# Loading order at the start of a fused Fourier and feed-forward kernel: first table behind x on SyncE, second tile on ScalarE's queue

## The chip, the cores and the metric

The kernel runs on one core of a Trainium2 chip. The metric is the time of one execution on the device, in microseconds (us); the time before is the median of 3 runs.

## The reference

```python
batch, seq, dim = (8, 3008, 256)               # x
X = np.fft.fft(x, axis=1)
X = np.fft.fft(X, axis=2)
x = X.real.reshape(24064, 256)
h = x @ w_in                                   # 256 x 2048
r = np.maximum(h, 0.0)
return (r * r @ w_out).astype(np.float32)      # 2048 x 256
```

## The kernel before

Each of 8 batches is a Fourier transform along 3008 rows and 256 columns, followed by two matrix products with a squared ReLU between them. The transform along the rows is a product with tables of cosines and sines. Symmetries make the tables small: the rows of x are regrouped on the host in sets of four mirrored rows (`x` has the shape batch, row, 4, 256), VectorE adds and subtracts the four ("folding"), and only a quarter of the rows is multiplied. The transform along the columns is folded into the first weights (`win`), so that a block of the steady loop multiplies the row transforms `Pt` and `Qt` with `G` (line 1101), forms and squares the ReLU on VectorE, ScalarE and GpSimd, and multiplies with the second weights (line 1166). That loop runs from about 40 us to the end.

The change lies in the head, which prepares batch 0. The rows are cut into seven tiles (`TILES`); tile t has a row of x in each partition, four vectors of 256 each. They are used in the order 0, `ODD0` (number 4), 1, 5, 2, 3, 6. For each, `load_x` brings x, `load_table` brings the cosines, `turn_table` makes the sines on ScalarE (line 234), `fold...` folds on VectorE, and `products_of` multiplies on TensorE (lines 811 and 824). Tile 0 has 95 rows in use and is loaded in two halves; its folding is `fold_first`: lines 583 and 584 for each half, 593 and 595 for both, while ScalarE makes turned copies for the first products (lines 588, 589, 591). Tile `ODD0` is loaded in two halves too; `fold_begun` uses the first in lines 604 and 605 and the second in line 606, then lines 607 and 609, and `fold_rest` goes on with lines 620 to 623. Later tiles are folded in lines 560 to 569.

The order of the work on each engine is the order in which the program is written out; nothing reorders it. SyncE's queue (SPq) issues nearly all loads, one after the other; ScalarE and GpSimd (POOL) have queues of their own, and an issue there stands in line with the engine's other instructions. The table `cosT` of tile 0 comes in three pieces of 32 rows (95 columns for each of two parities), the table of `ODD0` in one piece of 128 rows and 377 columns. Each DMA of SyncE and ScalarE completes on one of eight semaphores, which are taken in turn, and the DMA that takes one again is issued only when the one before it has landed.

`awake(n)` runs n products of a blank tile on TensorE (line 263; each shows as two records). `nc.scalar.copy(turn[0:1, 0, 0:1], ident[0:1, 0:1])`, line 1397, is ScalarE's first computation, ahead of which its function table is loaded; `nc.gpsimd.tensor_copy(turn[0:1, 0, 1:2], xt[0, 0][0:1, 3, 0:1])`, line 1398, makes GpSimd wait for tile 0 before it issues the table of tile 1 and the sines of tile 0.

Of the kernel before, what the change touches and what calls it, by code (L numbers as in the profile page):

```python
# [39 lines left out]
def row_tiles(S):  # L40

    q = S // 4
    tiles, at = [], 0
    for count in (q // 2 + 1, q // 2):
        assert 2 * P < count <= 3 * P
        for r in range(0, count, P):
            tiles.append((at + r, min(P, count - r)))
        at += count
    return tiles
# [35 lines left out]
def kernel(  # L85
# [12 lines left out]
    nc = tc.nc  # L98
# [42 lines left out]
    xt = {}  # L141
# [3 lines left out]
    ODD0 = NT - 3  # L145
# [15 lines left out]
    def later_rows(t):  # L161

        if t >= ODD0:
            return [(p, S // 8 + 1 + first, count, 1) for p, first, count in ODD[t - ODD0]]
        c, r0, step, rows = TILES[t]
        if t == TWO + 1:
            return [(p, TILES[TWO][1] + step * (2 * HALF2 - p - R), R, step) for p in range(0, ROWS2, R)]
        return [(0, r0, rows, step)]

    def load_x(b, t, parts_=4):  # L170
        if b and (t >= ODD0 or t == TWO + 1):
            xt[b, t] = xp.tile([P, 4, D], F32, name="xt", tag="x")
            for p, first, count, step in later_rows(t):
                nc.sync.dma_start(out=xt[b, t][p:p + count], in_=x[b, first:first + step * (count - 1) + 1:step])
            return
        c, r0, step, rows = TILES[t]

        if b == 0:
            rows, src = P, x.rearrange("b r i d -> (b r) i d")[r0:r0 + step * (P - 1) + 1:step]
        else:  # L180
            while rows % 15 and rows % 16 and r0 + step * rows < NROW:
                rows += 1
            src = x[b, r0:r0 + step * (rows - 1) + 1:step]

        pool, tag = (gp, "g") if b == 0 and t < NT - NX else (xp, "x")
        xt[b, t] = pool.tile([P, 4, D], F32, name="xt", tag=tag)
        for i in range(0, 4, parts_):
            nc.sync.dma_start(out=xt[b, t][0:rows, i:i + parts_],
                              in_=src[:, i:i + parts_])

    LATER = [(b, t) for b in range(1, B)
             for t in (TWO, TWO + 1, 0, *(() if b > 1 else (1,)), *range(ODD0, NL), *((1,) if b > 1 else ()))]
# [1 line left out]
    def load_later(i):  # L194
        if i < len(LATER):
            load_x(*LATER[i])
# [3 lines left out]
    cosT, sinT = ([const.tile([P, 2, WT], F32, name=nm), sp.tile([P, 2, WL], F32, name=nm + "l", tag="s")]  # L200
                  for nm in ("cosT", "sinT"))

    def part_of(tab, t):
        return tab[t in LATE]
# [3 lines left out]
    ident = const.tile([P, P], F32, name="ident")  # L208
# [5 lines left out]
    def load_table(tab, src, tiles, queue=nc.sync):  # L214

        for t in tiles:
            c, r0, step, rows = TILES[t]
            for i, (s0, count) in enumerate(row_tiles(S)):
                mine = [r for r in range(count) if (s0 + r - r0) % step == 0 and 0 <= (s0 + r - r0) // step < rows]
                if mine:  # L220
                    o, m = (s0 + mine[0] - r0) // step, len(mine)
                    while (step == 1 or m % 15) and m % 16 and o + m < P and mine[0] + step * m < P:
                        m += 1
                    nk = NC[0][c]
                    queue.dma_start(out=part_of(tab, t)[o:o + m, :, PLACE[t]:PLACE[t] + nk],
                                    in_=src[mine[0]:mine[0] + step * (m - 1) + 1:step, :, i, 0:nk])

    def turn_table(t):


        c, at, rows = TILES[t][0], PLACE[t], TILES[t][3]
        for kp in range(2):
            nk = NC[kp][c]
            nc.scalar.mul(part_of(sinT, t)[0:rows, kp, at:at + nk], part_of(cosT, t)[0:rows, kp, at:at + nk][:, ::-1],
                          sind[0:rows, 0, P - 1:])
# [24 lines left out]
    def awake(n):  # L260
        filled = psh.tile([P, CH], F32, name="filled", tag="h")
        for _ in range(n):
            nc.tensor.matmul(filled[:, 0:P], blank, blank, start=True, stop=True)
# [157 lines left out]
    turn = const.tile([P, 3, 4], F32, name="turn")  # L421
# [963 lines left out]
    def products_of(names):  # L1385
        for nm in names.split():
            (p_part if nm[0] == "P" else q_part)({"P": "", "Q": "", "E": "e"}[nm[0]] + nm[1:])

    start()
    load_table(cosT, cos_s, (0,), nc.scalar)  # L1390
    awake(11)
    load_x(0, 0, 2)
    load_x(0, ODD0, 2)
    load_table(cosT, cos_s, (ODD0,))
    load_x(0, 1)
    load_x(0, ODD0 + 1)
    nc.scalar.copy(turn[0:1, 0, 0:1], ident[0:1, 0:1])
    nc.gpsimd.tensor_copy(turn[0:1, 0, 1:2], xt[0, 0][0:1, 3, 0:1])
    load_table(cosT, cos_s, (1,), nc.gpsimd)
    load_table(sinT, sin_s, (0,), nc.gpsimd)  # L1400
# [12 lines left out]
    first = round_win(0, raw["in", 0])  # L1413
    fold_first()
    products_of("P0 E0")
    awake(2)
    turn_table(ODD0)
    fold_rest(ODD0, *fold_begun(ODD0))
    products_of("P4 E4 Q4")
# [219 lines left out]
    i = 0  # L1639
# [17 lines left out]
    for i in range(PLAIN, len(steps) + 2):  # L1657
        if i < len(steps):
            b, k0, n, j = steps[i]
# [130 lines left out]
```

## Time and profile before

| | |
|---|---|
| median of 3 runs | 1855.04 us (1854.84 to 1855.18) |
| profiled execution | 1855.63 us, span 1853.8 us |
| granted TensorE clock | 0.999 |
| DMA engines, mean | 70.10 MB, 38 GB/s |
| TensorE's first product, line 811 | at 6.46 us |

The profile shows one execution: times count from the start of the span, PE is TensorE, PEld its weight loads, DVE is VectorE, ACT ScalarE. A group of instructions is shown with its number, busy time and what ended the idle time before it. The time of the profiled execution is 1.83 us more than the span, and 0.59 us more than the median of the runs.

### The profile page before, as it was taken

The numbers are of one execution on the slowest core, as the hardware profiler recorded it, in microseconds if no ns is written. First come the engines' busy times: TensorE is split into PE (matmuls) and PEld (weight loads), VectorE is DVE, ScalarE is ACT, GpSimd is POOL, SyncE is SP. The second block draws the span as 40 slices with busy tenths as digits, with TensorE's granted clock in tenths as the row PEclk, the third lists the DMA queues.
The fourth block names the chain that finished last, engine by engine and source line by source line (L and its number), as shares of the span: only waits on it lengthen the run. The fifth ranks groups of instructions, "written<-read, shape, count | busy, mean of one in ns | idle before, by whom it ended". The sixth has DMA issues, their size and how long they took to land.

```text
span 1853.8 us, 33923 instructions
## 1 busy us (share of the span) xinstructions
PE 1846.4 (100%) x11336; PEld 1746.8 (94%) x11336; DVE 1473.9 (80%) x3481; ACT 1076.3 (58%) x1596; POOL 1458.5 (79%) x2132
## 2 busy tenths in 40 slices
PE   9999999999999999999999999999999999999999
PEld 7699999999999999999999999999999999999998
DVE  8998788887788878788788887788878887767666
ACT  5785555665556655657456664565645666444454
POOL 3499778788788887888778887788877888787885
PEclk9999999999999999999999999999999999999999
DMA  7441011110111101111011100111001100000010
GB/s 223 109 61 43 19 25 47 41 29 23 32 32 46 30 18 32 43 39 27 15 32 46 49 15 15 46 45 36 15 21 46 35 15 21 19 20 15 21 43 23
DMA packets 153987, 70.10 MB, mean 38 GB/s; under 512 B 132608, under 2 KB 144717, under 8 KB 153813
## 3 DMA queue, kind: packets, MB, share of 16 engines
q1 hardware_dynamic: 153173, 67.58, 14.4%
q8 instruction: 91, 1.49, 0.3%
q14 instruction: 83, 0.68, 0.1%
q10 hardware_dynamic: 384, 0.20, 0.0%
q0 software_dynamic: 256, 0.15, 0.0%
HBM read 43.18 MB, written 24.69 MB: 37 GB/s over the span
## 4 chain that ended last, share of the span: by engine, by line
PE 98%; DVE 1%; ACT 0%; DMA 0%; issue 0%; POOL 0%; SPq 0%; DVEq 0%; ACTq 0%
PE F L1166 34%; PE S L1166 23%; PE hQ L1101 17%; PE hP L1101 17%; PE pd L947 1%; PE mA L1195 1%; PE mB L1195 1%; PE pd L921 1%; PE pd L824 1%; PE pg L360 1%; PE ph L1069 0%; PE ph L1074 0%; PE fin L1277 0%; DMA xt<-in_x_dram 0%; DVE w L569 0%
## 5 line engine op out<-in xcount | busy, mean ns | idle before, releaser
L1114 ACT ACTIVATE g<-g 128x1008 f32<-128x1008 f32 (+1 forms) x384 | 399.4, 1040 | 303.2 <-DVE g L1110 278.5
L1105 DVE SCALAR_TENSOR_TENSOR he<-ew,gE,hP 128x252 f32<-128x252 f32 (+1 forms) x748 | 321.3, 471 | 284.6 <-PE hP L1101 284.5
L1117 ACT ACTIVATE g<-g 128x1008 f32<-128x1008 f32 (+1 forms) x384 | 399.4, 1040 | 12.0
L1101 PE MATMUL hQ<-Qt,G 128*128 128x252 f32 (+3 forms) x1496 | 378.7, 376 | 0.4 <-ACT g L1114 0.2
L1101 PE MATMUL hP<-Pt,G 128*128 128x252 f32 (+1 forms) x1496 | 378.1, 375 | 0.0
L1166 PE MATMUL F<-s,wsum 128*128 128x168 f32 (+1 forms) x1496 | 335.4, 306 | 0.0
L1101 PEld LDWEIGHTS hQ<-Qt,G 128*128 128x128 f32 (+1 forms) x1496 | 282.3, 190 | 36.2 <-ACT g L1114 2.0
L1166 PE MATMUL F<-g,wout 128*128 128x168 f32 (+1 forms) x1496 | 304.1, 305 | 0.0
L1139 POOL TENSOR_TENSOR s<-g 128x168 f32<-128x168 f32 (+1 forms) x187 | 101.3, 542 | 251.1 <-ACT g L1117 133.5
L1109 DVE TENSOR_TENSOR g<-he,hQ 128x504 f32<-128x504 f32 (+1 forms) x374 | 252.9, 676 | 39.3 <-DVE he L1105 2.7
L1101 PEld LDWEIGHTS hP<-Pt,G 128*128 128x128 f32 x1496 | 266.2, 190 | 17.6 <-issue 0.7
L1166 PE MATMUL S<-s,wout 128*128 128x168 f32 (+1 forms) x1496 | 280.3, 306 | 0.0
L1166 PE MATMUL S<-s,wsum 128*128 128x168 f32 (+1 forms) x1496 | 273.7, 306 | 0.0
L1166 PE MATMUL F<-g,wsum 128*128 128x168 f32 (+1 forms) x1496 | 273.5, 305 | 0.0
L1110 DVE TENSOR_TENSOR g<-he,hQ 128x504 f32<-128x504 f32 (+1 forms) x374 | 251.0, 671 | 0.0
L1166 PEld LDWEIGHTS F<-s,wsum 128*128 128x128 f32 x1496 | 247.5, 190 | 0.0
L1166 PEld LDWEIGHTS S<-s,wsum 128*128 128x128 f32 x1496 | 239.1, 190 | 8.5 <-issue 0.5
L1166 PEld LDWEIGHTS F<-g,wsum 128*128 128x128 f32 x1496 | 239.3, 190 | 8.1
L1166 PEld LDWEIGHTS F<-g,wout 128*128 128x128 f32 x1496 | 239.3, 190 | 0.0
L1166 PEld LDWEIGHTS S<-s,wout 128*128 128x128 f32 x1496 | 230.9, 190 | 0.7 <-issue 0.5
L1142 POOL TENSOR_TENSOR s<-s 128x336 f32<-128x336 f32 (+1 forms) x187 | 168.5, 901 | 14.7
L1145 POOL TENSOR_TENSOR s<-s 128x336 f32<-128x336 f32 (+1 forms) x187 | 167.8, 898 | 14.7
(246 smaller groups left out, 2474.6 us busy)
## 6 DMA issues: line engine op xcount, KB each, us to landing
out_dram<-os SPq DMA_DIRECT2D x376, 56.0 KB
xt<-in_x_dram SPq DMA_DIRECT2D x35, 384.0 KB
xt<-in_x_dram SPq DMA_DIRECT2D x63, 128.0 KB
raw<-in_moe_w_out_dram SPq DMA_DIRECT2D x20, 256.0 KB
ew<-e_dram SPq DMA_DIRECT2D x39, 126.0 KB
out_dram<-os SPq DMA_DIRECT2D x288, 7.0 KB
raw<-in_moe_w_in_dram SPq DMA_DIRECT2D x16, 256.0 KB
xt<-in_x_dram SPq DMA_DIRECT2D x5, 512.0 KB
```

What stands on the lines that cost most here:

```text
L360: nc.tensor.matmul(pg, tab[:, i], win[j][:, i], start=i == 0, stop=i == 1)
L1101: nc.tensor.matmul(to[:, h, 0:n], w[:, fs], v[:, ks], start=h == 0, stop=True, skip_group_check=True)
L1105: nc.vector.scalar_tensor_tensor(out=t[:, h, 0:n], in0=window[b, k0][:, 0:n], scalar=gE[:, fc:fc + 1], in1=hP[:, h, 0:n], op0=ALU.mult, op ...
L1109: tt(out=g[:, :, 0:n], in0=t[:, :, 0:n], in1=hQ[:, :, 0:n], op=ALU.add)
L1110: tt(out=g[:, :, n:2 * n][:, :, ::-1], in0=t[:, :, 0:n], in1=hQ[:, :, 0:n], op=ALU.subtract)
L1114: act(g[:, :, 0:2 * n], g[:, :, 0:2 * n], AF.Relu)
L1117: act(g[:, :, 0:2 * n], g[:, :, 0:2 * n], AF.Square)
L1139: gt(out=s[:, 11], in0=b2[:, 0], in1=b1[:, 0], op=SUB)
L1142: gt(out=s[:, 4:6], in0=s[:, 4:6], in1=s[:, 10:11].to_broadcast([P, 2, tb]), op=SUB)
L1145: gt(out=s[:, 6:9:2], in0=s[:, 2:4], in1=s[:, 6:8], op=ADD)
L1166: nc.tensor.matmul(acc[nm][:, slot, 0:tb], w, v, start=q == 0 and nm not in begun, stop=q == end - 1, skip_group_check=True)
L1195: nc.tensor.matmul(acc[nm][:, 0:2 * n], wout[:, j, h, c], g[:, c, 0:2 * n], start=j == c == 0, stop=j == NJ - 1 and c == 1)
```

## The change

In the head, tile 0 of x is loaded with 96 rows instead of 128. The first table's three pieces go from ScalarE's queue, where they were the first instructions, to SyncE's queue behind tile 0. ScalarE's first copy, and with it its function table, stands ahead of two DMAs that ScalarE now issues: the halves of tile `ODD0`, which SyncE issued before. The fillers ahead of the first products are 9 instead of 11, and the two ahead of the products of `ODD0` are left out.

```diff
-    def load_x(b, t, parts_=4):
+    def load_x(b, t, parts_=4, queue=nc.sync):
...
-        if b == 0:
+        if b == 0 and t:
             rows, src = P, x.rearrange("b r i d -> (b r) i d")[r0:r0 + step * (P - 1) + 1:step]
         else:
             while rows % 15 and rows % 16 and r0 + step * rows < NROW:
...
-            nc.sync.dma_start(out=xt[b, t][0:rows, i:i + parts_],
-                              in_=src[:, i:i + parts_])
+            queue.dma_start(out=xt[b, t][0:rows, i:i + parts_], in_=src[:, i:i + parts_])
...
     start()
-    load_table(cosT, cos_s, (0,), nc.scalar)
-    awake(11)
+    awake(9)
     load_x(0, 0, 2)
-    load_x(0, ODD0, 2)
-    load_table(cosT, cos_s, (ODD0,))
+    nc.scalar.copy(turn[0:1, 0, 0:1], ident[0:1, 0:1])
+    load_x(0, ODD0, 2, nc.scalar)
+    load_table(cosT, cos_s, (0, ODD0))
     load_x(0, 1)
     load_x(0, ODD0 + 1)
-    nc.scalar.copy(turn[0:1, 0, 0:1], ident[0:1, 0:1])
     nc.gpsimd.tensor_copy(turn[0:1, 0, 1:2], xt[0, 0][0:1, 3, 0:1])
...
     products_of("P0 E0")
-    awake(2)
     turn_table(ODD0)
```

## The prediction

> **What bounds the kernel now.** I read the page's busy shares and chain first, then the chain in order of time for the first 30 us, then stretches, the timeline and the DMA queues of the first 10 us.
>
> ```profile
> PE 1846.4 (100%) x11336; PEld 1746.8 (94%) x11336; DVE 1473.9 (80%) x3481; ACT 1076.3 (58%) x1596; POOL 1458.5 (79%) x2132
> PE 98%; DVE 1%; ACT 0%; DMA 0%; issue 0%; POOL 0%; SPq 0%; DVEq 0%; ACTq 0%
> ```
>
> TensorE is busy 1846.4 of 1853.8 us, so everything that is not matmul time amounts to 7.4 us, head and tail together. A change of the head can win only part of that.
>
> The chain, in order of time (start, length, what):
>
> ```profile
> 0.75 0.41 SPq L188
> 1.22 4.32 DMA xt<-in_x_dram
> 5.56 0.42 DVE fs L583
> ...
> 7.37 0.33 DVE fs L604
> 7.70 0.34 DVE fd L605
> 8.04 0.35 DVE fs L606
> ```
>
> Until 5.56 the end is set by the second half of x's first tile (called x0b here; x0a is the first half, x4a and x4b are the halves of the tile ODD0, which is number 4). From 5.56 to about 23.5 VectorE folds tile after tile without a gap, then GpSimd's fold of the last tile and its conversion of weights release TensorE at 28.19. From 39 us on TensorE alone counts. So the step that can move the end is when VectorE may start, and whether it then runs on. In the stretches (PE, PEld, DVE, ACT, POOL busy, then clock, DMA share, GB/s):
>
> ```profile
> 2.00:4.00 2.00, 2.00 (x12) 2.00 (x10) 0.00 (x0) 1.47 (x2) 1.69 (x5) 1.00 0.86 234
> 4.00:6.00 2.00, 1.78 (x10) 1.59 (x9) 1.20 (x4) 0.00 (x0) 0.74 (x5) 1.00 0.95 336
> 6.00:8.00 2.00, 1.54 (x12) 1.46 (x13) 1.86 (x7) 0.96 (x4) 2.00 (x5) 1.00 1.07 410
> 10.00:14.00 4.00, 4.00 (x18) 2.59 (x17) 3.90 (x10) 1.16 (x5) 0.00 (x0) 1.00 1.07 302
> 18.00:22.00 4.00, 3.63 (x19) 2.79 (x18) 3.93 (x11) 0.97 (x4) 0.00 (x0) 1.00 1.10 364
> ```
>
> VectorE is full from 6 us, the DMA engines from 2 us: what goes first delays what comes after. The timeline of the issues (start, length):
>
> ```profile
> 0.75 1.38 ACTq L225 DMA_DIRECT2D cosT<-in_cos_s_dram  x3
> 0.75 1.83 SPq L188 DMA_DIRECT2D xt<-in_x_dram  x4
> 2.16 1.28 ACT L1397 ACT_TABLE_LOAD   x1 [2.16 <-issue]
> 6.42 0.52 PEld L811 LDWEIGHTS pd<-cosT,fs 95*128 95x128 f32 x4 [0.83 <-DVE fd L584]
> 6.43 0.28 ACT L588 ACTIVATE tp<-cosT 95x94 f32<-95x94 f32 x1 [2.79 <-DMA cosT<-in_cos_s_dram]
> 8.04 1.11 ACT L234 ACTIVATE sinT<-cosT,sind 128x377 f32<-128x377 f32 x2 [0.66 <-DMA cosT<-in_cos_s_dram]
> ```
>
> The three pieces of the first table, issued by 2.13, are in only at 6.43, just when the first product could start; the table of ODD0 is in at 8.04. The two queues of 2 to 4 us (packets, MB, share):
>
> ```profile
> q1 hardware_dynamic: 233, 0.43, 74.8%
> q10 hardware_dynamic: 121, 0.04, 11.7%
> ```
>
> ScalarE's queue (q10) moves a third of the packets with a tenth of the bytes, at a total of 234 GB/s; once it is empty, from 6 us, the total is 410.
>
> **The change, part by part.** Its sum is made against the profiled execution, 1855.63 us (span 1853.8 and 1.83 around it), which is 0.59 above the median of 1855.04; the difference is then put on the median. All but the head keeps its instructions and order.
>
> *x0 first and smaller.* 96 of 128 rows: 384 KB instead of 512, and no table beside it. Today x0's 512 KB have passed q1 at about 4.35 (0.45 MB by 4.0, 0.56 by 4.5, summed over half-microseconds) and x0b is used at 5.56, 1.2 later. At the same 234 GB/s without the table, 0.39 MB have passed by 3.6, so x0b is in at 4.75, 0.8 early. Bounds: 128 KB less at 336 GB/s alone gives 0.4; a queue that runs at once at 336 gives 1.2. I take 0.8, since the slow first microseconds are in the 234. VectorE's start goes to 4.75 and its line 606, which needs x4b, could start 2.4 us later as now (5.56 to 7.96), at 7.15.
>
> *The first table on SP behind x0.* Three issues of about 0.45 us move from ScalarE to SP, so SP issues the table from 1.65 to 3.0 and ODD0's table until 3.7 (0.69 now). The table's 240 packets took 3.9 us beside x; behind x0 they take 0.9 to 1.7 us (240 at 60 to 110 ns on 16 engines: what is left of the engines' time in 4.4 to 5.0 and in 2.6 to 4.2 when each packet of x counts 62 ns, as at 6.0, where 52 passed alone in 0.2 us). That is 4.5 to 5.3, landed at 5.4 to 6.2, against a first product that could start at 5.6. No loss: it ends between 0.2 and 1.0 earlier than 6.43. The issue of tile 1 no longer waits for a table piece (0.67 idle before 3.98) and goes at 3.7; that of tile 5 waits for x0a and goes at about 4.1.
>
> *x4's halves on ScalarE.* The table load (1.28) starts at 0.75 in place of 2.16, the copy of 0.19 follows, so x4a is issued at 2.3, where SP has it at 1.65 now. Landing takes 3.4 us from the issue for x0a, so 5.7; line 604 wants it at 6.5. It is covered, by 0.8. The built program's order shows an added wait: each DMA completes on one of eight semaphores in turn, and x4b gets that of x0b, so ScalarE holds x4b back until x0b has landed, at 4.75. Behind it on ScalarE stands the copy for the first products (line 588), which waits for the table beyond 5.4 anyway, so the wait costs that nothing. But x4b itself, issued at 2.1 today and in well before 7.96, is now issued 2.65 us later. First packets come 0.95 to 1.3 us after an issue (1.7 on q1, 2.05 on q10, both issued at 0.75), so at 5.75 to 6.05; its 256 KB take 0.65 us at 400 GB/s if they run alone, 1.3 at half the share and 2.0 at a third; the landing is about 1.1 behind. In: 7.5, 8.1, 9.1. At that time SP's ring holds the end of ODD0's table and then two tiles of 512 KB in 4 KB packets. I take about 7.9, between alone and half: the summed work ahead of tile 1 (first table 0.9 to 1.7, x4a 0.65, ODD0's table 0.95, from 3.7) lasts until 6.2 to 7.0, so x4b meets mostly ODD0's table.
>
> Line 606 then starts at about 7.9, now 7.96: VectorE's 0.8 us are spent waiting in front of it, and all that follows is shifted by -0.05. The ends are 7.15 (-0.8) and 9.1 (+1.1). [...]
>
> *Fewer fillers.* 8 of the 26 records go from TensorE: 4 before the first product, in time in which TensorE waits anyway, and 4 (0.47 us, 8.92 to 9.39) before the products of ODD0, which wait for VectorE's line 609 until 9.37 now. Nothing is saved by that; the clock is a rival below.
>
> *Downstream.* Tile 1, tile 5 and the later loads come 128 KB sooner at 0.36 to 0.41 MB/us, some 0.3 us; tile 1 is wanted at 10.6, tile 5 at 13.3 (in at 11.15). GpSimd's own table loads wait for x0b and start 0.8 earlier. No stall moves there. Sum: -0.8 and +0.75, so 1855.58 for a profiled execution and 1854.99, or 1855.0, for the median.
>
> **Rivals.**
> *The gain stays.* x4b runs nearly alone and is in before 7.3: line 606 starts at 7.15 to 7.3. For it: little stands on SP's ring if the table is quick. Against: first packets not before 5.75. -0.7: 1854.3.
> *x4b shares with tile 1 (slower).* If SP's ring has reached the 4 KB packets, or x0b lands late (5.2), x4b gets a third and is in at 9.0. It decides from a landing later than 7.96 on, and each us beyond costs VectorE, GpSimd and the end one. For it: q10 had a third of the packets in 2 to 4 us. +1.0: 1856.0.
> *The clock stays low (slower).* Fillers measure these busy times (mean ns) in 4.5 to 5.0 and 5.5 to 6.0:
>
> ```profile
> L263 PE MATMUL filled<-blank 128*128 128x128 f32 x4 | 1.1, 421 | 0.0
> L263 PE MATMUL filled<-blank 128*128 128x128 f32 x3 | 0.5, 278 | 0.0
> ```
>
> So TensorE became faster at about 5.2, after 4.1 us of work, although the granted clock reads 1.00 throughout. 18 records of 0.214 us now end at 4.9, ahead of that point. If it stays slow (0.214 against 0.118 per filler, x1.8) until the end of the first product group, nothing is lost: that group has time. If it lasts through ODD0's products (9.39 to 13.20), they take 3.1 us more, of which the idle of 10 to 28.2 (0.7 us) takes some back: +2.4 at most, half of that if the clock opens midway. For it: the gap moves in front of the opening. Against: 3.85 of 4.1 us of work remain and the real products follow 0.7 us later. About +1.3: 1856.3. [...]
> *The change doesn't do what it says:* the order shows each moved issue where the text has it, so that is out.
>
> **How the numbers follow.** Forecast (-0.4 to +0.4) 0.42, gain stays 0.22, sharing 0.20, clock 0.14, something else 0.02. The forecast is 1855.0, its own range 1854.6 to 1855.4. The range goes from 1854.2 (the gain kept) to 1856.6 (sharing, and most of the clock). 0.2% is 3.7 us, about what a measurement of this kernel can tell from no change; no case reaches it but the unknown one and stacked late cases: faster 0.02, same 0.94, slower 0.04.
>
> **What would show it.** x0b: line 583's second start at 4.4 to 5.1. x4b: line 606 (605 after) waits for x's DMA, 0.3 to 1.2 us, and starts at 7.5 to 8.3. First product at 5.5 to 6.2. ScalarE's table load at 0.8. TensorE's release at 28.1 to 28.3, and all of it shifted alike until the end. Wrong would be a start of TensorE's weights stage that does not follow line 606, ODD0's products above 0.4 us each in spacing, or a difference that arises after 39 us.

## The result and the profile after

The changed kernel takes 1859.33 us (median of 13 runs, 1857.92 to 1859.99); the kernel before, in 13 runs beside it, 1855.36 (1854.84 to 1855.68). The ratio is 1.0021 with a 95% interval of 1.0013 to 1.003: slower by 4.0 us. The profiled execution took 1859.18 us, span 1857.4, which is 3.55 above the profiled one of before.

The chain of the changed kernel in order of time (start, length, what), which in the kernel before went from the DMA to line 583 at 5.56:

```profile
1.20 3.34 DMA xt<-in_x_dram
4.56 6.36 DMA xt<-in_x_dram
10.95 0.44 DVE fs L605
...
42.24 0.69 PE ph L1068 x2
```

A second DMA stands in the chain now: the second half of tile ODD0 (x4b), issued at 4.56 and landed at 10.92. Line 605 (606 before) starts at 10.95 instead of 7.96. The timeline shows what went as forecast around it:

```profile
0.74 1.28 ACT L1391 ACT_TABLE_LOAD   x1 [0.74 <-PEq L1773]
1.35 0.38 ACTq L188 DMA_DIRECT2D xt<-in_x_dram  x1
4.56 0.34 ACTq L188 DMA_DIRECT2D xt<-in_x_dram  x1
4.57 0.42 DVE L582 TENSOR_TENSOR fs<-xt 95x256 f32<-95x256 f32 x1 [0.55 <-DMA xt<-in_x_dram]
5.90 0.28 ACT L587 ACTIVATE tp<-cosT 95x94 f32<-95x94 f32 x1 [3.67 <-DMA cosT<-in_cos_s_dram]
5.92 1.14 PE L810 MATMUL pd<-cosT,fs 95*128 95x95 f32 x4 [0.65 <-DVE sc L592]
6.30 0.41 DVE L603 TENSOR_TENSOR fs<-xt 128x256 f32<-128x256 f32 x1
10.95 0.43 DVE L605 TENSOR_TENSOR fs<-xt 128x256 f32<-128x256 f32 x1 [3.90 <-DMA xt<-in_x_dram]
12.22 2.88 PE L823 MATMUL pd<-cosT,w 128*128 128x377 f32 x4 [1.75 <-DVE w L608]
```

The same work in the kernel before:

```profile
6.46 0.66 PE L811 MATMUL pd<-cosT,fs 95*128 95x95 f32 x4 [0.67 <-DVE fd L584]
7.96 0.42 DVE L606 TENSOR_TENSOR fs<-xt 128x256 f32<-128x256 f32 x1
9.39 1.43 PE L824 MATMUL pd<-cosT,w 128*128 128x377 f32 x4
38.89 0.69 PE L1069 MATMUL ph<-Pt,G 128*128 128x252 f32 x2 [0.21 <-ACT G L367]
```

Tile 0's second half (x0b) is in at 4.57, a full us early, and the first table at 5.90. x4b is issued at the moment x0b is in: in the trace its issue names semaphore 103 twice, as the one that it waits for and as its own; x0b, issued at 1.20, has the same one, and the last update of x0b's landing there is at 4.54. The traces show the same of the other loads: the 1027 DMAs of SyncE and ScalarE carry eight numbers in either kernel (101, 103 to 108 and 110; in the kernel before 100, 102 and 104 to 109), and of the 1019 that take a number again, 1012 are recorded with a wait for it. VectorE stands still for 3.90 us in front of line 605. And the products of ODD0, when they come, take 0.67 us each (12.22 to 14.90 for four) where they took 0.32 (9.39 to 10.66). TensorE was slow before the wait already: its first four products took 1.14 us where they took 0.66, and in this execution it became fast only at 16.9.

The stretches of the changed kernel (busy PE, PEld, DVE, ACT, POOL, then clock, DMA share, GB/s):

```profile
4.00:6.00 2.00, 1.35 (x7) 1.08 (x6) 1.31 (x5) 0.10 (x1) 1.72 (x6) 1.00 0.90 235
6.00:8.00 2.00, 2.00 (x10) 2.00 (x11) 1.05 (x4) 1.14 (x5) 2.00 (x5) 1.00 1.01 340
8.00:10.00 2.00, 2.00 (x11) 2.00 (x11) 0.00 (x0) 0.83 (x2) 0.33 (x1) 1.00 1.01 369
10.00:14.00 4.00, 2.25 (x6) 1.41 (x6) 2.91 (x9) 0.73 (x3) 0.00 (x0) 1.00 1.09 312
```

VectorE does nothing from 8 to 10 us, while the DMA engines are full. The DMA queues (packets, MB, share), first for 4.5 to 7.0 and then for 7.0 to 9.0:

```profile
q1 hardware_dynamic: 418, 0.70, 99.9%
q10 hardware_dynamic: 8, 0.01, 1.1%
...
q1 hardware_dynamic: 137, 0.49, 62.5%
q10 hardware_dynamic: 109, 0.22, 34.0%
```

For 2.6 us after its issue x4b hardly moves (the 8 packets of q10 are the end of the first half, before 5.0); then it passes packet beside packet with SyncE's queue, 109 to 137, but those are larger (3.6 KB on average against 2.0), so it has a third of the bytes. From there the delay runs on: TensorE's first weights stage starts at 31.65 instead of 28.19, the last product that waits for ScalarE ahead of the steady loop (line 1068, 1069 before) starts at 42.24 instead of 38.89, and after it nothing more is lost but 0.2 us.

### The profile page after: what moved, and what is told of

Same layout as the page of the kernel before. It is cut to its first block, busy times and chain, and to the rows that moved or that the text cites. A ratio compares the mean times of both kernels' runs of the same rounds, so it can differ in the third digit from the quotient of the medians.

```text
span 1857.4 us, 33907 instructions
## 1 busy us (share of the span) xinstructions
PE 1848.8 (100%) x11328; PEld 1749.0 (94%) x11328; DVE 1474.6 (79%) x3481; ACT 1075.9 (58%) x1596; POOL 1457.8 (78%) x2132
## 4 chain that ended last, share of the span: by engine, by line
PE 97%; DVE 1%; DMA 1%; ACT 0%; SPq 0%; issue 0%; DVEq 0%; ACTq 0%
PE F L1165 34%; PE S L1165 23%; PE hQ L1100 17%; PE hP L1100 17%; PE pd L946 1%; PE mA L1194 1%; PE mB L1194 1%; PE pd L920 1%; PE pd L823 1%; DMA xt<-in_x_dram 1%; PE pg L359 0%; PE ph L1068 0%; PE fin L1276 0%; PE ph L1073 0%; DMA xe<-in_x_dram 0%; DVE w L568 0%
## 5 line engine op out<-in xcount | busy, mean ns | idle before, releaser
L1141 POOL TENSOR_TENSOR s<-s 128x336 f32<-128x336 f32 (+1 forms) x187 | 168.5, 901 | 14.7
L1144 POOL TENSOR_TENSOR s<-s 128x336 f32<-128x336 f32 (+1 forms) x187 | 167.7, 897 | 14.7
```

Source lines behind the costliest of these rows:

```text
L1141: gt(out=s[:, 4:6], in0=s[:, 4:6], in1=s[:, 10:11].to_broadcast([P, 2, tb]), op=SUB)
L1144: gt(out=s[:, 6:9:2], in0=s[:, 2:4], in1=s[:, 6:8], op=ADD)
```

## The experiments

Theory L: x4b is late, because it is held for a semaphore and then passes beside the large packets of tiles 1 and 5. Theory C: TensorE stays at its slow rate because fillers are missing. Parts of C may come with L, since the late half leaves TensorE idle. All times are medians, with the kernel before run beside them in brackets.

**Without the hold.**

```diff
-    nc.scalar.copy(turn[0:1, 0, 0:1], ident[0:1, 0:1])
     load_x(0, ODD0, 2, nc.scalar)
+    nc.scalar.copy(turn[0:1, 0, 0:1], ident[0:1, 0:1])
```

> The changed kernel with ScalarE's copy behind the two halves of tile ODD0, by which the second half takes a semaphore that nothing uses yet, so both halves are issued by 1.5; fewer fillers stay. Theory L: the second half lands at 5.5 to 7, tile 0 some tenths later than in the changed kernel as both pass together, VectorE waits under 0.6 us on the second half, time 1854.8 to 1856.3. Theory C: above 1857.5.

1855.79 us (1855.12), interval of the ratio 0.9995 to 1.0014. x4b is not waited for at all (line 605 at 8.11); tile 0 comes later, 5.70. 3.3 of the 4.0 us are gone with all of the rest of the change, the fewer fillers too: the issue that is held is needed for the loss. (The edit also brings the first half forward, from 1.35 to 0.75.)

**The halves on SyncE**, between the two tables.

```diff
-    load_x(0, ODD0, 2, nc.scalar)
-    load_table(cosT, cos_s, (0, ODD0))
+    load_table(cosT, cos_s, (0,))
+    load_x(0, ODD0, 2)
+    load_table(cosT, cos_s, (ODD0,))
```

> The changed kernel with the halves of tile ODD0 issued by SyncE, between the first table and ODD0's table; fewer fillers stay. Theory L: the second half is in by 7.5, VectorE does not wait 3.9 us there, and the time is 1854.7 to 1856.3. Theory C: TensorE stays slow as in the changed kernel, and the time is above 1857.5.

1855.86 (1855.12), 0.9994 to 1.0012. Line 605 starts at 6.38, 1.6 us before the kernel before, and then VectorE waits 1.7 us for tile 1, until 10.77 (10.62 before). What tile 0 wins is taken back by the next load.

**All fillers back.**

```diff
-    awake(9)
+    awake(11)
...
     products_of("P0 E0")
+    awake(2)
```

> The changed kernel with all fillers again (11, and 2 ahead of ODD0's products). Theory L (the second half of tile ODD0 comes late: held back for a semaphore, then beside 4 KB packets): VectorE's second half of that tile still starts near 10.95, and of the loss of 4.0 us about 3.0 stay, 1858.2 to 1858.9. Theory C (TensorE stays at its slow rate because fillers are missing): the products run at the fast rate from about 5.2 on and the loss is gone but for a rest, below 1856.3.

1859.00 (1855.12), 1.0012 to 1.003, just above theory L's range: the loss stays, so the missing fillers are not its cause. The trace shows a slow TensorE all the same, but by another way than in the changed kernel. With all fillers it was fast by 6.7. Line 605 started at 11.55, TensorE had nothing from 9.1 to 12.9, and then ODD0's products took 0.53 us each, at a granted clock of 0.86 in 12 to 14 and 0.50 in 14 to 16. The two fillers, 0.64 us of work, didn't bridge that gap of 3.8 us.

**Fewer fillers alone**, in the kernel before (9, and none ahead of ODD0's products).

> The kernel before with the fewer fillers alone (9, none ahead of ODD0's products). Theory L: at most 1 us over before, 1855.3 to 1856.4, VectorE's folds where they were. Theory C: most of the loss is here, above 1858, with 377-column products at 0.63 us each for several us.

1855.42 (1855.12), 0.9992 to 1.0012: by itself this costs nothing that can be told apart. The runs spread over 1.7 us (1854.69 to 1856.38), and in the profiled one (1856.34) ODD0's products were slow until 14.7 and VectorE waited 1.1 us for TensorE later on.

**Tiles 1 and 5 behind the halves.**

```diff
-    load_x(0, 1)
-    load_x(0, ODD0 + 1)
+    nc.sync.dma_start(out=cosd, in_=cos_d.rearrange("(c p) m -> p c m", p=P))
+    load_x(0, 1, 4, nc.scalar)
+    load_x(0, ODD0 + 1, 4, nc.scalar)
```

> The changed kernel with tiles 1 and 5 (4 KB packets) issued on ScalarE's queue behind the halves of ODD0, in place of SyncE's, which brings a table of 128 KB for later and tile 5's table instead. The second half of ODD0 is still held until tile 0 is in (4.5). Theory S (the late landing comes from sharing the DMA engines with the 4 KB packets of tiles 1 and 5): it lands by 8.7, two us before the changed kernel's 10.9. Theory H (the hold and what the issue itself takes decide): 10 or later. Tile 1 comes late for its fold in both, so the time says little: 1857 to 1861.

1856.85 (1854.95), a little under the range expected. x4b is still held until x0b is in, but lands 2.6 us sooner. The timeline of VectorE, and TensorE's products of ODD0:

```profile
6.55 0.43 DVE L603 TENSOR_TENSOR fs<-xt 128x256 f32<-128x256 f32 x1 [0.73 <-DMA xt<-in_x_dram]
8.37 0.43 DVE L605 TENSOR_TENSOR fs<-xt 128x256 f32<-128x256 f32 x1 [1.06 <-DMA xt<-in_x_dram]
9.65 1.53 PE L823 MATMUL pd<-cosT,w 128*128 128x377 f32 x4 [1.70 <-DVE w L608]
```

So the hold with this company costs some tenths (8.37 against 7.96). Of the 2.6 us, 0.6 come from an earlier issue: tile 0 was in by 4.01, half a us sooner, and x4b was issued at 3.93. Then 2.6 us went by until its first packet at 6.5, as in the changed kernel (4.56 to 7.2), but the packets passed in 1.3 us instead of 2.5, and the landing was 0.6 behind them instead of 1.1. So theory S holds for the passing, where the 4 KB packets were beside it. The wait ahead of the first packet is as long without them. The edit is not pure, since the first half was held too here (issued at 3.33) and stood ahead of x4b on its queue; so what fills that wait stays open.

**Work for TensorE in the gap.** As with all fillers back, but 18 ahead of ODD0's products.

> The changed kernel with 11 fillers and 18 ahead of ODD0's products, in place of 9 and none, so TensorE has work while it waits for the late half (8.4 to about 12). If TensorE's slow rate after that gap has a part in the loss: ODD0's products run at 0.32 us each from the start and the time is 0.5 to 1.2 us below the changed kernel's, 1858.0 to 1858.8. If VectorE's late folds alone set it: no change, 1859.0 to 1859.6.

1858.01 (1854.95), 1.001 to 1.0029. ODD0's products take 0.32 us each from the start. In the profiled execution line 605 came at 9.70, 1.74 late, the product of line 1068 at 40.62, 1.73 late, and the time was 1.86 over the profiled one of before: with the clock at 1.00 from 8 to 16 us, TensorE followed VectorE one to one. In the changed kernel those three are 2.99, 3.35 and 3.55. The slow rate has thus a part of about 0.4 (3.35 less 2.99) in that execution of the changed kernel; the medians are 0.9 apart (3.06 and 3.97 over before), but their intervals overlap.

**The clock without the late half.** The run without the hold, with `awake(17)` for `awake(9)`.

> The run without the hold (ScalarE's copy behind the halves of ODD0, all issued by 1.65), with 17 fillers in place of 9, so that TensorE has work until its first table is in (6.8). There the granted clock fell to 0.50 from 9.6 to 13.4 and the median was 0.7 over before. If that idle time closes the clock: the granted clock stays 1.00 up to 16 us, ODD0's products take 0.32 us each, and the time is 0.3 to 0.9 below, 1854.8 to 1855.4. If fillers make no difference: 1855.6 to 1856.0 again.

1855.38 (1854.99), and the spread shrinks from 1.5 us to 0.55 (1855.17 to 1855.72). The stretches, with 9 fillers and then with 17:

```profile
8.00:10.00 2.00, 2.00 (x15) 1.83 (x14) 1.90 (x7) 0.98 (x3) 1.46 (x3) 0.81 0.92 287
10.00:12.00 2.00, 2.00 (x4) 1.01 (x3) 1.97 (x6) 0.00 (x0) 0.00 (x0) 0.50 1.01 323
```

```profile
8.00:10.00 2.00, 2.00 (x16) 1.79 (x15) 1.90 (x7) 1.00 (x3) 1.40 (x3) 1.00 0.95 320
10.00:12.00 2.00, 2.00 (x8) 1.19 (x7) 1.97 (x6) 0.00 (x0) 0.00 (x0) 1.00 1.02 336
```

With 9 fillers an idle gap of 1.57 us ahead of the first product (5.27 to 6.84) was followed by a fall of the clock to 0.50, from 9.2 to 12.6; with 17 it stayed at 1.00. The medians are 0.3 to 0.4 us apart, which their intervals don't tell from nothing. The two profiled executions, one with the fall and one without, took 1855.35 and 1855.36, with line 1068 at 39.03 and 39.01. So where VectorE is on time no cost of this fall is shown.

**ODD0 in one DMA**, issued at 1.35, with 11 fillers and 6 ahead of ODD0's products.

```diff
-    load_x(0, ODD0, 2, nc.scalar)
+    load_x(0, ODD0, 4, nc.scalar)
```

> The changed kernel with tile ODD0 in one DMA of 512 KB on ScalarE's queue, which takes a semaphore that nothing has used, so all of it is issued at 1.35; 11 fillers, and 6 ahead of ODD0's products. Theory L (hold and sharing made the half late): it lands at 5.5 to 7.0, VectorE waits under 0.7 us for it, and 3 to 4.5 us of the loss are gone, 1854.5 to 1856.0. If ScalarE's queue is slow in itself, whatever the hold: landing above 8.5, 1857 and more.

1857.86 (1855.10), 1854.87 to 1858.64, interval 1.0002 to 1.0019: missed, though ODD0 is in time (lines 603 and 605 at 7.98 and 8.65 without a wait). Its 512 KB took the engines from tile 0's second half and the first table, as the queues of 4.0 to 5.0 show:

```profile
q10 hardware_dynamic: 88, 0.35, 90.0%
q1 hardware_dynamic: 33, 0.02, 7.6%
```

x0b came at 6.25 and the table at 7.38, TensorE was idle for 1.91 us, and its clock was 0.50 from 8 to past 14, with line 1068 at 42.10. VectorE was only 0.7 late, and TensorE has no idle time from 8 to 38 us, so here the slow clock would be most of the loss. That is argued from one trace; no run sets it apart, and that the spread of 3.8 us between runs of the same program comes from the clock is not shown either.

**On the way to a better version.** The halves on SyncE with 11 and 6 fillers:

> The halves of ODD0 on SyncE between the two tables (as in the run of that name) with 11 fillers and 6 ahead of ODD0's products. TensorE is at the fast rate for ODD0's products (0.32 us each). Theory: the loads bound this head (VectorE waited 1.7 us for tile 1 until 10.77, now 10.6), so time is near before: 1854.8 to 1855.5, and less spread than without the fillers (1855.2 to 1856.4). If the slow rate had no part: as without them, 1855.9.

1855.74 (1854.95), above the range and with no less spread (1854.88 to 1856.27); ODD0's products at 0.32 us each, but tile 1 came at 11.75 in the profiled execution. The same with 96 rows for tiles 1, 2 and 3 (`if b == 0 and rows > 96:`):

> The same with 96 rows instead of 128 for tiles 1, 2 and 3 too (128 KB less each). If the loads bound the head: tile 1 is in 0.3 us sooner, later tiles up to 0.9, and the time is 0.3 to 0.9 below the run with all rows, 1854.2 to 1854.8, below before. If VectorE or TensorE bound it: no change.

1855.89 (1854.95): no gain in time, though tile 1 came sooner, at 10.99. The kernel before with 96 rows for tile 0 alone (`if b == 0 and t:`), and then for tiles 1, 2 and 3 too:

> The kernel before with 96 rows for tile 0, nothing else of the change. If tile 0's arrival sets the head: x0b 0.2 to 0.5 us early, and the time 0.1 to 0.5 below before. If the next load is late then: no change, within 0.1.

> The same with 96 rows for tiles 1, 2 and 3 as well, 512 KB less up to the weights. Every load is earlier, tile 1 by 0.6 us; the time is 0.2 to 0.6 below before, at or below the run with tile 0 alone.

1854.70 (1855.10), interval 0.9989 to 1.0007, and 1855.48 (1855.10), 0.9994 to 1.0012. The first is the lowest median of all, 0.4 below before, but the interval holds 1. Its VectorE, ahead of the kernel before from line 583 on, loses part of it at tile 1:

```profile
6.95 0.43 DVE L606 TENSOR_TENSOR fs<-xt 128x256 f32<-128x256 f32 x1
9.88 0.69 DVE L560 TENSOR_TENSOR fs<-xt 94x512 f32<-94x512 f32 x1 [0.19 <-DMA xt<-in_x_dram]
```

With 96 rows for all, tile 1 comes at 10.61, 0.73 later than with 128, as the engines moved 251 GB/s in 8 to 10 us where they moved 364. The pair with the halves on SyncE shows the same (245 against 361 in 8 to 10), at engines busy all the time, though there tile 1 still came sooner. Fewer bytes did not always mean an earlier landing; why the rate fell is open.

## Why the prediction was wrong

**x0 first and smaller** held: 4.75 forecast, 4.57 measured. **The first table behind x0** held: 5.4 to 6.2 forecast, 5.90 measured, and the first product at 5.92. **x4a** was forecast at 2.3, behind the function table; it was issued at 1.35, beside that load. Its issue did not stand in line behind the table's load and the copy (2.04), as had been taken. The error was harmless, since line 603 did not wait.

**x4b** is the step that failed. The hold and its end were right (4.75 forecast, 4.56 measured). The landing was taken at 7.9, within 7.5 and 9.1, and was 10.92. Of its three terms the first was mis-sized: 0.95 to 1.3 us from the issue to the first packet came from the first issues of the kernel before, and with a table and two tiles already issued on SyncE's queue it was 2.6. (4.75 and 0.95 make 5.70, not the 5.75 of the prediction; nothing hangs on it.) The second, the passing, was taken between alone and half the share; it was a third and took 2.5 (7.2 to 9.7), more than the 2.0 of my bound, which held the full rate of 400 GB/s. The third, 1.1 to 1.2 behind, was right. I had read a third of the packets in the very rows of the kernel before and still took the milder case, because I let x4b meet the end of ODD0's table; it met the 4 KB packets. Without them beside it the passing took 1.3. The landing also differs between executions: 9.70, 10.95 and 11.55 for the same loads.

How two queues divide the engines between them is not shown by these runs. ScalarE's and SyncE's queue passed 109 and 137 packets in 7 to 9 us of the changed kernel, but 88 and 33 in 4 to 5 us of the run with one DMA, and in the wait of 2.6 us some 400 packets of SyncE's queue went by before the first one of x4b.

**Fewer fillers** had been a rival by itself, and its sign came: in the changed kernel TensorE was slow from the first product to 16.9, and so it was until past 14 in the kernel before with fewer fillers. But it is not the 4 us. With all fillers TensorE became fast in time, and then the late half made the idle gap of 3.8 us, after which the clock fell to 0.50 (14 to 16 us): the loss was the same. Nor do 9 fillers always leave it slow: in three other runs with 9 (halves on SyncE, without the hold, tiles 1 and 5 behind) its products were fast by 6.9 at the latest. Alone, fewer fillers cost nothing that can be told from noise (0.3 in the kernel before); beside the late half the slow rate adds about 0.4 in the profiled execution, and 0.9 between medians whose intervals overlap. Idle gaps of 1.39, 1.57 and 1.91 us (halves on SyncE, without the hold, one DMA) were followed by a granted clock of 0.50. The length of the gap alone does not decide it: after the 1.70 us in the run with tiles 1 and 5 behind, the clock stayed at 1.00.

**The rivals and the range** failed at one point: sharing (+1.0) and clock (+1.3) were set out as two ways of which one would come. They came together and the first was three times as large, 3.0. The rule that each us of x4b costs the end one held: what line 605 lost (2.99) is lost at the end (3.55) but for the clock's part and 0.2 after 42 us. That no stall moves to tile 1 was not put to the test in the changed kernel, where x4b came later still; with the halves on SyncE it did move there, 1.7 us.

## What to carry to other kernels

In these runs a transfer's price had a part before its first packet, about 1 us for the first issues of the kernel before and 2.6 us for x4b, with a table and two tiles issued before it: read it from a transfer that was issued behind as much, not from the first ones of the program. When an order of loads is changed, look up which semaphore each DMA takes over and issue the loads wanted first where nothing holds them. Rivals that can come together, such as a late load and a slow TensorE, are to be priced together.

## What the runs showed of the hardware

- ScalarE's queue issued a DMA at 1.35 while its function table was loading (0.74 to 2.02).
- A granted clock of 1.00 is shown from the start also where products take twice their time: in the changed kernel 0.63 us per 377-column product until 16.8, under a clock of 1.00. In these traces it reads 0.50 only after a fall, so before the first change the products' own spacing is the measure.
- 512 KB on ScalarE's queue left SyncE's 33 packets of 121 in a microsecond (4.0 to 5.0), and x0b, issued before it (1.21 against 1.36), was in at 6.25 instead of 4.57.
